# A spectral transform loop in pairs: first-stage products, second stages and mixes of two units grouped

## The chip, the cores and the metric

The kernel runs on one core of a Trainium2 chip. The metric is the device time of one execution in microseconds (us); the time given is the median of several runs. Engines are named as in the profile: PE (TensorE), DVE (VectorE), ACT (ScalarE), POOL (GpSimd) and SP (SyncE, which here issues all DMAs).

## What is computed

A spectral layer with a soft threshold, followed by a gated feed-forward network (FFN). x is 8 x 3136 x 256, the hidden width 1024, all in float32.

```python
X = np.fft.rfft(x, axis=1)
Yr = X.real @ w_r - X.imag @ w_i + b_r
Yi = X.real @ w_i + X.imag @ w_r + b_i
Y = soft(Yr, 0.01) + 1j * soft(Yi, 0.01)   # sign(v) * max(|v| - 0.01, 0)
y = np.fft.irfft(Y, n=3136, axis=1)
h = np.maximum(y @ w_in, 0)
c = depthwise convolution of h along the sequence with conv_w (3 taps)
out = (h / (1 + np.exp(-c))) @ w_out
```

## The kernel before

The sequence of 3136 is 49 x 64, and the transform goes through DRAM between its factors. The **first stage** (`stage1_pe`, L333; copies L350 on ACT and L351 on DVE; stores L338 and L342) does the 49-point part in tile products, 8 for each of the 8 batches, 64 in all; each is four matmuls with 49 x 64 weights, in the four quadrants of the PE array, into two PSUM banks. The first 8 come before the loop. The **unit** is what the loop runs over: 4 of the 24 frequencies of one batch, 6 units a batch, and two units more for an edge frequency of four batches each: 50 units, numbered 0 to 49. For each unit:

- `stage2` (L384): the 64-point part, 8 matmuls over the whole array (16 records in the profile) into two PSUM banks of the unit's `ps_s2`, from the tile a2 (L371, a DMA from the first stage's scratch). For each bank ACT copies one part (d, L387) and rounds both (fh, L388), DVE subtracts (d, L389) and takes the remainder (fl, L390). fh and fl are a value's rounded part and remainder, so that products in float32r keep float32 accuracy.
- `third`: the third plane of fh and fl, from d: ACT rounds it (L395), GpSimd takes the remainder (L396).
- `mix` (L412): the complex product with w_r and w_i in three real ones, planes 2, 0 and 1 of fh and fl in this order, 12 matmuls of 128 x 256 each (rounded x high weights, rounded x low, remainder x high), into three banks `ps_mx`; DVE adds bias and planes into v (L415, L417).
- `shrink` (L428, L429 on ACT, L430 on GpSimd) or `clip` (L422, L423 on DVE): the soft threshold, v to r.
- `stage3_pe` (L440, L443): the inverse 64-point part in quadrants, 8 matmuls (16 records), into `ps_s3`, a PSUM tile of two banks of which there is one buffer (pool psa); `stage3_out` (L450 on ACT, then a DMA store L455).

`ps_s1`, `ps_s2`, `ps_mx` and the fourth stage's tiles take their banks in turn from one pool of six (psx). The **fourth stage** (`last_stage`, `stage4`, L159, L168, L170) does the inverse 49-point part. For batch 0 its 8 pieces stand at the end of this loop; for the others they stand in the FFN.

Beside that, a generator (`background`) splits the FFN weights and taps into two float32r parts: some ten small DVE steps a piece (L264 to L280) and one ACT cast (L278). It advances one step each time it is called, three times a unit from unit 8 to 43.

The loop runs over `it` from 0 to 53 (n_it is 50, LAG 4). The order in which the code stands is the order in which each engine gets its instructions: the loop is under a manual schedule, while the FFN behind it is ordered by a scheduler. An iteration takes, in this order: the DMAs of x, tables and a2; third stage of unit it - 4; one or two first-stage products (1, 2, 1, 1, 2, 1 in turn); second stage of unit it; shrink of unit it - 2; `third` of unit it; fourth stage in iterations 45 to 48; mix of unit it - 1. Unit 49 calls `third` ahead of the shrink. Iterations 50 to 53 drain: fourth stage, third stage, clip and the last mix.

```python
psx = ab.enter_context(tc.tile_pool(name="psx", bufs=6, space=PSUM))
psa = ab.enter_context(tc.tile_pool(name="psa", bufs=1, space=PSUM))
...
            if it < n_it:
                xs[it] = stage2(items[it][1], a2s.pop(it))
...
            if 0 <= it - 1 < n_it:
                vs[it - 1] = mix(xs.pop(it - 1))
```

The FFN (from 467 us on) multiplies up (L650) and down (L678) with three float32r products each, and ACT and DVE do the gate between them.

Of the kernel before, what the change touches and what calls it, by code (L numbers as in the profile page):

```python
# [26 lines left out]
UG = 4  # L27
# [84 lines left out]
def spectral_ffn_kernel(ctx: ExitStack, tc: tile.TileContext, x, w_r, w_i, b_r, b_i,  # L112
# [61 lines left out]
    with ExitStack() as ab:  # L174
# [63 lines left out]
        def load_inv1(g):  # L238
            if g < NG:
                sl = slice(g * UG // 2, (g + 2) * UG // 2)  # L240
                nc.sync.dma_start(i1[:, 0, sl], inv1v[:, sl])
            else:
                nc.sync.dma_start(i1[:, :, U // 2], inv1v[:, U // 2:])
# [152 lines left out]
            nc.gpsimd.tensor_tensor(fl[:, :, 2], d, fh[:, :, 2].bitcast(F32), op=ALU.subtract)  # L396
            return fh, fl

        def mix(xs):


            fh, fl = xs
            ps = {c: psx.tile([K2, UG // 2, D], F32, name=f"ps_mx{c}", tag="bank") for c in (2, 0, 1)}
            for c in (2, 0, 1):
                q = (1, 2, 0)[c]
                for k in range(UG // 2):
                    mm = []
                    for t in range(NT):
                        a = [f[:, t, c, 2 * k:2 * k + 2, :] for f in (fh, fl)]
                        mm += [(a[0], wmix_hi[:, t, q, :]), (a[0], wmix_lo[:, t, q, :]), (a[1], wmix_hi[:, t, q, :])]  # L410
                    for n, (lt, rh) in enumerate(mm):
                        nc.tensor.matmul(ps[c][:, k, :], lt, rh, start=(n == 0), stop=(n == len(mm) - 1))  # L412
            v = wk.tile([K2, 2, UG // 2, D], F32, name="v")
            for c in range(2):
                nc.vector.tensor_tensor(v[:, c], ps[2], bias[:, c:c + 1, :].to_broadcast([K2, UG // 2, D]), op=ALU.add)  # L415
            for c in range(2):
                nc.vector.tensor_tensor(v[:, c], ps[c], v[:, c], op=ALU.add)  # L417
            return v

        def clip(v):  # L420
# [51 lines left out]
        LAG, WP0, LATE, NW, NF0, NF1 = 4, 8, 10, 7, 14, 3  # L472
        xs, vs, ss, a2s, xq, pair = {}, {}, {}, {}, {}, []
        p1 = nx = NX

# [8 lines left out]
        def next_s1(p):  # L484
            return stage1_pe(xq[p // 2][:, p % 2])
# [68 lines left out]
        Y0, Y1 = n_it - 6, n_it - 1  # L554
        jgs = iter(range(NPC))

        def one_by_one():
# [10 lines left out]
            stage4(jg, z2, y0, one_by_one)  # L568
            ask_z2()

        for it in range(n_it + LAG):
            drain = it >= n_it
            if it:
                fetch(1)
            if 2 < it + 2 < NG and it % 2 == 0:
                load_t2(it + 2)
            elif it == LATE:
                load_t2(NG)
                load_inv1(NG)
# [5 lines left out]
            if drain:  # L585
                last_stage()
            if it >= LAG:
                g3 = items[it - LAG]
                ps3 = stage3_pe(g3[1], ss.pop(it - LAG))
            n_s1 = min(2 if 0 < it < 5 else (1, 2, 1, 1, 2, 1)[(it - 5) % 6] if it else 0, n_pc - p1)  # L590
            ps1 = [next_s1(p1 + i) for i in range(n_s1)] if it > 1 else []
            if it >= LAG:
                stage3_out(*g3, ps3)
            if WP0 <= it < Y0:
                next(background, None)
            elif it == WP0 - 2:
                next(background)
            for ps in ps1:
                stage1_out(p1, ps)
                p1 += 1  # L600
            ask_a2(it + 1)
            if WP0 <= it < Y0:
                for _ in range(2):
                    next(background, None)
            if it < n_it:
                xs[it] = stage2(items[it][1], a2s.pop(it))
            if it == Y0:
# [6 lines left out]
            if it == n_it - 1:  # L614
                xs[it] = third(xs[it])
            if 0 <= it - 2 < n_it:
                ss[it - 2] = (clip if drain else shrink)(vs.pop(it - 2))
            if it < n_it - 1:
                xs[it] = third(xs[it])
            if Y0 < it < Y1:  # L620
                last_stage()
            if it == 1:
                for _ in range(n_s1):
                    stage1_out(p1, next_s1(p1))
                    p1 += 1
            if 0 <= it - 3 < NG:
                fill_inv1(it - 3)
            if 0 <= it - 1 < n_it:
                vs[it - 1] = mix(xs.pop(it - 1))
# [109 lines left out]
```

## Time and profile before

| | |
|---|---|
| median of 3 runs | 1681.46 us (1679.61 to 1683.54) |
| the profiled execution | 1678.42 us, span 1676.6 us |
| PE busy | 1662.8 us, 99% of the span |
| DVE busy | 1389.2 us, 83% |
| ACT busy | 1177.0 us, 70% |
| POOL busy | 192.4 us, 11%, all in the transform loop |
| mean granted PE clock | 0.997 |

Times in the trace count from the start of the span. A matmul's end is modelled and matmuls overlap, so a busy PE need not be one at its peak: what a piece of PE work costs is read from the start of its first matmul to the start of the next piece's first. A row of the timeline has start, duration, engine, line, operation, what it writes and reads, shapes, and how many equal ones follow each other (x16); in brackets the idle time before it and what ended it. The loop begins at about 33 us and its last matmul on PE is at about 467 us.

### The profile page before, as it was taken

The page shows a single profiled execution, that of the slowest core. Times are in us where ns is not written, and L with a number is a line of the kernel's source. Part 1 is how long each engine was busy: PE and PEld are TensorE (multiplying, and loading weights), DVE is VectorE, ACT ScalarE, POOL GpSimd, SP SyncE. Part 2 cuts the span into 40 slices and gives each one's busy share as a digit, 9 for nine tenths or more (in the row PEclk, how much of TensorE's full clock was granted, in tenths as well). Part 3 has the DMA queues.
Part 4 walks back from the last instruction along what each step waited for, and adds up shares of the span by engine and source line. Part 5 has one row for each costly group of instructions (what it writes and reads, how often), then busy time and mean ns, then how long its engine had stood idle before and what let it go on. Part 6 is the DMA issues. An engine that isn't in the chain of part 4 may idle for free.

```text
span 1676.6 us, 30666 instructions
## 1 busy us (share of the span) xinstructions
PE 1662.8 (99%) x12618; PEld 1543.9 (92%) x12618; DVE 1389.2 (83%) x1728; ACT 1177.0 (70%) x1585; POOL 192.4 (11%) x114
## 2 busy tenths in 40 slices
PE   9899999999999999999999999999999999999998
PEld 6788888889999999999999999999999999999998
DVE  3578888877688888888888888888888888888887
ACT  3577777777677677767676776767677676776776
POOL 1444444445300000000000000000000000000000
PEclk9899999999999999999999999999999999999999
DMA  8999999876421101111110111111001111100001
GB/s 239 279 279 291 270 261 269 254 225 186 110 79 44 49 32 42 52 52 42 52 49 26 42 39 33 42 51 52 32 33 52 52 35 49 42 23 23 23 23 45
DMA packets 108297, 162.29 MB, mean 97 GB/s; under 512 B 10842, under 2 KB 87806, under 8 KB 108094
## 3 DMA queue, kind: packets, MB, share of 16 engines
q1 hardware_dynamic: 108158, 160.34, 32.2%
q8 instruction: 100, 1.64, 0.4%
q14 instruction: 39, 0.32, 0.1%
HBM read 83.24 MB, written 77.07 MB: 96 GB/s over the span
## 4 chain that ended last, share of the span: by engine, by line
PE 97%; DMA 1%; SPq 1%; issue 1%; ACT 0%; ACTq 0%
PE ps_h L650 33%; PE acc L678 33%; PE ps_mx L412 13%; PE ps_s L159 7%; PE ps_s L384 6%; PE ps_s L333 3%; PE ps_s L440 3%; DMA hx<-in_x_dram 1%; SPq L316 0%; DMA a<-sch 0%; PE ps_s L443 0%; DMA sch<-ha 0%; SPq L319 0%; SPq L347 0%; ACT o L684 0%
## 5 line engine op out<-in xcount | busy, mean ns | idle before, releaser
L659 DVE SCALAR_TENSOR_TENSOR c<-h,cw,c 128x896 f32<-128x896 f32 x448 | 512.8, 1147 | 67.5 <-ACT c L657 66.2
L678 PE MATMUL acc<-wout,gh 128*128 128x256 f32 x3136 | 567.6, 281 | 0.4 <-ACT gh L664 0.4
L650 PE MATMUL ps_h<-yh,win 128*128 128x450 f32 x1792 | 549.1, 367 | 0.0
L678 PEld LDWEIGHTS acc<-wout,gh 128*128 128x128 f32 x3136 | 491.0, 188 | 6.4 <-ACT gh L664 0.6
L678 PE MATMUL acc<-wout,gl 128*128 128x256 f32 x1568 | 435.6, 280 | 0.0
L652 ACT ACTIVATE h<-ps_h 128x900 f32<-128x900 f32 x224 | 207.4, 926 | 234.3 <-PE ps_h L650 234.3
L650 PEld LDWEIGHTS ps_h<-yh,win 128*128 128x128 f32 x1792 | 338.7, 189 | 26.1 <-issue 0.4
L650 PE MATMUL ps_h<-yl,win 128*128 128x450 f32 x896 | 329.4, 368 | 0.0
L678 PEld LDWEIGHTS acc<-wout,gl 128*128 128x128 f32 x1568 | 293.2, 188 | 0.2
L661 DVE TENSOR_TENSOR c<-h,c 128x896 f32<-128x896 f32 x224 | 243.4, 1087 | 47.6 <-ACT c L660 46.6
L665 DVE TENSOR_TENSOR gl<-c,gh 128x896 fp32r<-128x896 f32 x224 | 243.0, 1088 | 34.4 <-ACT gh L664 30.4
L664 ACT CAST gh<-c 128x896 fp32r<-128x896 f32 x224 | 210.4, 944 | 77.0 <-DVE c L661 77.0
L660 ACT ACTIVATE c<-c 128x896 f32<-128x896 f32 x224 | 213.4, 953 | 28.4 <-DVE c L659 25.9
L650 PEld LDWEIGHTS ps_h<-yl,win 128*128 128x128 f32 x896 | 169.0, 189 | 11.3
L657 ACT ACTIVATE c<-h,cw 128x896 f32<-128x896 f32 x168 | 175.5, 1044 | 2.9 <-DVE gl L665 0.2
L412 PE MATMUL ps_mx<-wmix_hi,fh 128*128 128x256 f32 x600 | 172.5, 288 | 0.0
L412 PE MATMUL ps_mx<-wmix_lo,fh 128*128 128x256 f32 x600 | 167.9, 280 | 0.0
L412 PE MATMUL ps_mx<-wmix_hi,fl 128*128 128x256 f32 x600 | 167.4, 279 | 0.0
L430 POOL TENSOR_TENSOR r<-r,v 128x1024 f32<-128x1024 f32 x48 | 114.6, 2388 | 218.9 <-ACT v L429 200.1
L384 PEld LDWEIGHTS ps_s<-t,a 128*128 128x128 f32 (+1 forms) x800 | 94.7, 194 | 37.4 <-issue 23.3
L159 PEld LDWEIGHTS ps_s<-i,z 98*128 98x128 f32 x1024 | 122.4, 192 | 2.0 <-issue 0.8
L159 PE MATMUL ps_s<-i,z 98*128 98x98 f32 x1024 | 123.3, 273 | 0.0
(93 smaller groups left out, 1672.7 us busy)
## 6 DMA issues: line engine op xcount, KB each, us to landing
z<-sc SPq DMA_DIRECT2D x64, 392.0 KB
sc<-z SPq DMA_DIRECT2D x96, 256.0 KB
out_dram<-o SPq DMA_DIRECT2D x27, 896.0 KB
xr<-in_x_dram SPq DMA_DIRECT2D x112, 192.0 KB
sc<-a SPq DMA_DIRECT2D x56, 384.0 KB
a<-sc SPq DMA_DIRECT2D x42, 512.0 KB
hx<-in_x_dram SPq DMA_DIRECT2D x16, 192.0 KB
a<-sch SPq DMA_DIRECT2D x6, 512.0 KB
```

What stands on the lines that cost most here:

```text
L159: nc.tensor.matmul(to, z2[:, j, t * P:(t + 1) * P], i2[:, 0 if jg or j else 1, :], start=(j == 0), stop=(j == JG - 1), skip_group_check=True)
L384: nc.tensor.matmul(ps[:, k], a2[0:kk, k, t * P:(t + 1) * P], t2[0:kk, q, :], start=(k == 0), stop=(k == UG - 1), skip_group_check=True)
L412: nc.tensor.matmul(ps[c][:, k, :], lt, rh, start=(n == 0), stop=(n == len(mm) - 1))
L650: nc.tensor.matmul(ps[:, a, 0:CH + 2], lt, rh, start=(n == 0), stop=(n == len(mm) - 1))
L652: nc.scalar.activation(h, ps[:, :, 0:CH + 2], AF.Relu)
L657: nc.scalar.mul(c, h[:, :, 0:CH], cw[:, 0, f:f + 1])
L659: nc.vector.scalar_tensor_tensor(c, h[:, :, k:k + CH], cw[:, k, f:f + 1], c, op0=ALU.mult, op1=ALU.add)
L660: nc.scalar.activation(c, c, AF.Sigmoid)
L661: nc.vector.tensor_tensor(c, h[:, :, 1:CH + 1], c, op=ALU.mult)
L664: nc.scalar.copy(gh, c)
L665: nc.vector.tensor_tensor(gl, c, gh.bitcast(F32), op=ALU.subtract)
L678: nc.tensor.matmul(acc[m // 2][:, m % 2, :], lt[:, sl], rh[:, f, :], start=(f == 0 and n == 0 and m % 2 == 0), stop=(f == NF - 1 and n == ...
```

## The change

Units 0 to 7 run as before. From unit 8 on, an iteration takes units u and u + 1 (u = 8, 10, ... 48). In order: DMAs of two x loads and of a2; third stage of u - 4; up to two first-stage products; third stage of u - 3; the third product, if there is one; second stage and `third` of u, then of u + 1; shrink of u - 1; mix of u; shrink of u; mix of u + 1. Iteration 8 also does the mix of unit 7, which was left over. The six calls of `background` that two units had are spread over the pair. Iterations 46 and 48 have a fourth stage behind each second stage. In a pair's mixes (`paired`) the planes go 0, 2, 1, and the four DVE additions are regrouped: bias to planes 0 and 2 first, then plane 2 and plane 1. The drain is third stage, fourth stage, third stage and so on for units 46 to 49, and only unit 49 uses clip.

```diff
-        def mix(xs):
+        def mix(xs, paired=False):
...
-            ps = {c: psx.tile([K2, UG // 2, D], F32, name=f"ps_mx{c}", tag="bank") for c in (2, 0, 1)}
-            for c in (2, 0, 1):
+            order = (0, 2, 1) if paired else (2, 0, 1)
+            ps = {c: psx.tile([K2, UG // 2, D], F32, name=f"ps_mx{c}", tag="bank") for c in order}
+            for c in order:
...
+            if paired:
+                biased(0, 0)
+                biased(1, 2)
+                joined(0, 2)
+                joined(1, 1)
+            else:
...
-        for it in range(n_it + LAG):
+        for it in range(PAIR):
...
+        for u in range(PAIR, n_it, 2):
+            busy = u < Y0
+            fetch(2)
...
+            ask_a2(u + 2)
+            n_s1 = min(sum((1, 2, 1, 1, 2, 1)[(i - 5) % 6] for i in (u, u + 1)), n_pc - p1)
...
+            z = s3(u - LAG)
+            out1 = pieces(min(n_s1, 2))
+            next(out1)
+            if busy:
+                steps(2)
+            stage3_out(*z)
+            next(out1, None)
+            z = s3(u + 1 - LAG)
+            out1 = pieces(max(n_s1 - 2, 0))
+            next(out1)
+            stage3_out(*z)
+            next(out1, None)
+            if busy:
+                steps(1)
+            ask_a2(u + 2)
+            if u == PAIR:
+                ss[u - 2] = shrink(vs.pop(u - 2))
+                vs[u - 1] = mix(xs.pop(u - 1))
+            for i in (u, u + 1):
+                xs[i] = third(stage2(items[i][1], a2s.pop(i)))
+                if i == u:
+                    ask_a2(u + 3)
+                if u > Y0:
+                    last_stage()
...
+            ss[u - 1] = shrink(vs.pop(u - 1))
+            if busy:
+                steps(1)
+            vs[u] = mix(xs.pop(u), True)
+            ss[u] = shrink(vs.pop(u))
+            if busy:
+                steps(2)
+            vs[u + 1] = mix(xs.pop(u + 1), True)
+
+        for n in range(2):
+            z = s3(n_it - LAG + n)
+            last_stage()
+            stage3_out(*z)
+            if n == 0:
+                ss[n_it - 1] = clip(vs.pop(n_it - 1))
+            last_stage()
+        for n in range(2):
+            stage3_out(*s3(n_it - 2 + n))
```

`s3(i)` is the third stage of unit i, `pieces(n)` issues n first-stage products and, called again, their copies and stores, and `steps(n)` calls `background` n times. Two places show how the instructions move. The first is PE in the middle of the loop, before, from one third stage to the next second stage, twice (ps_s<-r is a third stage, ps_s<-xr a first-stage product, ps_s<-t a second stage; the 36 matmuls of a mix are left out between them):

```order
862 L440 MATMUL ps_s_2643<-r,i_465 64x256 x8
863 L333 MATMUL ps_s_2652<-xr,f_118 64x512 x2
864 L333 MATMUL ps_s_2653<-xr,f_118 64x512 x2
865 L333 MATMUL ps_s_2658<-xr,f_118 64x512 x2
866 L333 MATMUL ps_s_2659<-xr,f_118 64x512 x2
867 L384 MATMUL ps_s_2690<-t_122,a_2436 128x128 x4
868 L384 MATMUL ps_s_2699<-t_122,a_2436 128x128 x4
...
905 L440 MATMUL ps_s_2766<-r,i_465 64x256 x8
906 L333 MATMUL ps_s_2775<-xr,f_118 64x512 x2
907 L333 MATMUL ps_s_2776<-xr,f_118 64x512 x2
908 L384 MATMUL ps_s_2796<-t_122,a_2542 128x128 x4
909 L384 MATMUL ps_s_2805<-t_122,a_2542 128x128 x4
```

And after, from the first third stage of a pair to its last second stage; the two mixes follow:

```order
857 L453 MATMUL ps_s_2592<-r,i_465 64x256 x8
858 L333 MATMUL ps_s_2601<-xr,f_118 64x512 x2
859 L333 MATMUL ps_s_2602<-xr,f_118 64x512 x2
860 L333 MATMUL ps_s_2607<-xr,f_118 64x512 x2
861 L333 MATMUL ps_s_2608<-xr,f_118 64x512 x2
862 L453 MATMUL ps_s_2627<-r,i_465 64x256 x8
863 L333 MATMUL ps_s_2636<-xr,f_118 64x512 x2
864 L333 MATMUL ps_s_2637<-xr,f_118 64x512 x2
865 L384 MATMUL ps_s_2654<-t_122,a_2361 128x128 x4
866 L384 MATMUL ps_s_2663<-t_122,a_2361 128x128 x4
867 L384 MATMUL ps_s_2679<-t_122,a_2454 128x128 x4
868 L384 MATMUL ps_s_2688<-t_122,a_2454 128x128 x4
```

The quadrant work of two units (third and first stages) stands together, and so does the work on the whole array. The second place is ACT, before, from the copy of a third stage (z) through the second stage's copies (d, fh) and the shrink (r, v) to the third plane (fh<-d):

```order
223 L450 COPY z_2781<-ps_s_2766 128x1024
224 L350 COPY a_2674<-ps_s_2775 128x2x256
225 L387 COPY d<-ps_s_2796 128x256
226 L388 CAST fh<-ps_s_2796 128x512
227 L387 COPY d<-ps_s_2805 128x256
228 L388 CAST fh<-ps_s_2805 128x512
229 L428 ACTIVATE r<-v,small 128x1024
230 L429 ACTIVATE v<-v,small 128x1024
231 L395 CAST fh<-d 128x2x256
```

And after, from the first second stage of a pair on:

```order
363 L387 COPY d<-ps_s_4383 128x256
364 L388 CAST fh<-ps_s_4383 128x512
365 L387 COPY d<-ps_s_4392 128x256
366 L388 CAST fh<-ps_s_4392 128x512
367 L395 CAST fh<-d 128x2x256
368 L387 COPY d<-ps_s_4408 128x256
369 L388 CAST fh<-ps_s_4408 128x512
370 L387 COPY d<-ps_s_4417 128x256
371 L388 CAST fh<-ps_s_4417 128x512
372 L395 CAST fh<-d 128x2x256
373 L441 ACTIVATE r<-v,small 128x1024
374 L442 ACTIVATE v<-v,small 128x1024
```

The third plane of a unit now stands right behind its second stage, ahead of the other unit's copies and of the shrink; a second shrink and the pair's copies of third and first stages follow.

More of the change, by code (lines that the diff above doesn't have):

```diff
@@ L413, in mix, with biased, joined @@
             v = wk.tile([K2, 2, UG // 2, D], F32, name="v")
[L414 to L417, printed above, removed]
+            def biased(c, src):
+                nc.vector.tensor_tensor(v[:, c], ps[src], bias[:, c:c + 1, :].to_broadcast([K2, UG // 2, D]), op=ALU.add)
+            def joined(c, src):
+                nc.vector.tensor_tensor(v[:, c], ps[src], v[:, c], op=ALU.add)
+            if paired:
[4 more added lines that the diff above has]
+            else:
+                for c in range(2):
+                    biased(c, 2)
+                for c in range(2):
+                    joined(c, c)
             return v
@@ L553, in spectral_ffn_kernel @@
         background = later()
-        Y0, Y1 = n_it - 6, n_it - 1
+        Y0 = n_it - 6
         jgs = iter(range(NPC))
@@ L569, in last_stage, with steps, s3, pieces @@
             ask_z2()
-        for it in range(n_it + LAG):
-            drain = it >= n_it
+        def steps(n):
+            for _ in range(n):
+                next(background, None)
+        def s3(i):
+            b, g = items[i]
+            return b, g, stage3_pe(g, ss.pop(i))
+        def pieces(n):
+            nonlocal p1
+            todo = [next_s1(p1 + i) for i in range(n)]
+            yield
+            for ps in todo:
+                stage1_out(p1, ps)
+                p1 += 1
+        for it in range(PAIR):
             if it:
@@ L584, in spectral_ffn_kernel @@
                 fill_t2(it + 1)
-            if drain:
-                last_stage()
             if it >= LAG:
[L588 to L591, printed above, removed]
-            if it >= LAG:
[L593 to L597, printed above, removed]
@@ L598, in spectral_ffn_kernel @@
-            for ps in ps1:
-                stage1_out(p1, ps)
-                p1 += 1
-            ask_a2(it + 1)
[L602 to L607, printed above, removed]
+                z = s3(it - LAG)
+            n_s1 = 2 if 0 < it < 5 else (1, 2, 1, 1, 2, 1)[(it - 5) % 6] if it else 0
+            if it > 1:
+                out1 = pieces(n_s1)
+                next(out1)
@@ new lines, in spectral_ffn_kernel @@
+            if it >= LAG:
+                stage3_out(*z)
+            if it == WP0 - 2:
+                steps(1)
+            if it > 1:
+                next(out1, None)
+            ask_a2(it + 1)
+            xs[it] = stage2(items[it][1], a2s.pop(it))
+            if it >= 2:
+                ss[it - 2] = shrink(vs.pop(it - 2))
+            xs[it] = third(xs[it])
+            if it == 1:
+                out1 = pieces(n_s1)
+                next(out1)
+                next(out1, None)
+            if 0 <= it - 3 < NG:
+                fill_inv1(it - 3)
@@ L613, in spectral_ffn_kernel @@
                     ask_z2()
[L614 to L629, printed above, removed]
+            ss[u - 1] = shrink(vs.pop(u - 1))
+            if busy:
+                steps(1)
+            vs[u] = mix(xs.pop(u), True)
[6 more added lines that the diff above has]
+            last_stage()
+            stage3_out(*z)
+            if n == 0:
[3 more added lines that the diff above has]
+            stage3_out(*s3(n_it - 2 + n))
         assert p1 == n_pc and not z2s and next(background, True)
```

17 lines of the change are left out of this document (13 added, 4 removed).

## Prediction

> **What bounds the kernel now.** I read four views: the chain that ended last, TensorE's waits, the windows by stage, and then the timeline of single units, engine by engine. The page's chain puts nearly the whole span on TensorE (PE):
>
> ```profile
> PE 97%; DMA 1%; SPq 1%; issue 1%; ACT 0%; ACTq 0%
> ```
>
> PE's own waits, over the whole trace (line, releaser, total us, times, longest), are all in the first 60 us but for the fourth, 0.4 us later on; these are the first and the third:
>
> ```profile
> PE ps_s L333 <- issue: 7.1, 3, 5.4
> ...
> PE ps_s L384 <- DMA a<-sch: 0.6, 1, 0.6
> ```
>
> The windows give busy time by stage (length, PE, PE weight loads, DVE, ACT, POOL, granted clock, DMA share, GB/s):
>
> ```profile
> core 0: us, PE busy (x) PEld busy (x) DVE busy (x) ACT busy (x) POOL busy (x), PEclk, DMA share, GB/s
> ...
> 44.40:54.70 10.30, 6.97 (x27) 5.39 (x28) 5.15 (x10) 2.11 (x5) 0.84 (x2) 0.50 1.01 279
> ...
> 60.00:372.00 312.00, 312.00 (x2923) 262.35 (x2920) 258.46 (x445) 232.07 (x361) 143.92 (x79) 1.00 0.91 265
> 372.00:408.00 36.00, 36.00 (x341) 32.91 (x340) 28.72 (x55) 26.57 (x40) 17.03 (x10) 1.00 0.63 175
> ...
> 467.00:1676.60 1209.60, 1204.87 (x8290) 1160.12 (x8288) 1040.43 (x1099) 859.36 (x1072) 0.00 (x0) 1.00 0.13 41
> ```
>
> From 60 us on PE is never idle in the transform loop, DVE is at 83% (258.46 of 312) and ACT at 74%. So the change can gain only where PE itself spends time between instructions, and it can lose wherever its new order makes PE wait for another engine. The FFN part after 467 us is the same work and full of PE; I take no change there. The timeline of PE shows what a unit costs; of the mix (L412) only the ends stand here:
>
> ```profile
> 285.07 0.28 PE L412 MATMUL ps_mx<-wmix_lo,fh 128*128 128x256 f32 x1
> 285.19 0.27 PE L412 MATMUL ps_mx<-wmix_hi,fl 128*128 128x256 f32 x1
> 285.39 1.11 PE L440 MATMUL ps_s<-r,i 64*64 64x256 f32 x16
> 286.31 1.91 PE L333 MATMUL ps_s<-xr,f 49*64 49x512 f32 x16
> 288.15 2.05 PE L384 MATMUL ps_s<-t,a 128*128 128x128 f32 x16
> 289.96 0.36 PE L412 MATMUL ps_mx<-wmix_hi,fh 128*128 128x256 f32 x1
> 290.16 0.28 PE L412 MATMUL ps_mx<-wmix_lo,fh 128*128 128x256 f32 x1
> 290.27 0.28 PE L412 MATMUL ps_mx<-wmix_hi,fl 128*128 128x256 f32 x1
> ...
> 294.33 1.11 PE L440 MATMUL ps_s<-r,i 64*64 64x256 f32 x16
> 295.25 1.05 PE L333 MATMUL ps_s<-xr,f 49*64 49x512 f32 x8
> 296.23 2.05 PE L384 MATMUL ps_s<-t,a 128*128 128x128 f32 x16
> ```
>
> I read start to start: third stage 0.92, first stage 1.84 for two tile products (16 records) and 0.98 for one, second stage 1.81, mix 4.37 us (289.96 to 294.33).
>
> **What the pairing removes.** Third and first stage run in quadrants of the array (64*64), second stage and mix on all of it. Going over costs time: the last mix step to the third stage takes 0.20 (285.19 to 285.39) where two mix steps are 0.12 apart, so 0.08. A second tile product adds 1.84 - 0.98 = 0.86, so of the 0.98 of a single one 0.12 is the way back to the whole array. Units without a first stage say the same, their third stage takes 1.04 to the second stage instead of 0.92:
>
> ```profile
> 377.84 1.11 PE L440 MATMUL ps_s<-r,i 64*64 64x256 f32 x16
> 378.88 2.05 PE L384 MATMUL ps_s<-t,a 128*128 128x128 f32 x16
> ```
>
> A unit goes over and back once; a pair now does so once. 21 pairs (units 8 to 49) save 21 x (0.08 + 0.12) = 4.2 us. Second stage to second stage and mix to mix keep their usual steps, as does second stage to mix now (0.03 and 0.20 instead of 0.11 and 0.12).
>
> On this price the Trainium skill has a rule: TensorEngine Tiling, Key Properties, says that changing the tiling mode drains TensorE. The rows above show 0.08 and 0.12 us for it; a full drain is the rival that ends faster, below.
>
> **What it adds, first: the third plane is due early.** In the mix of unit u the planes are now taken in the order 0, 2, 1, right behind both second stages. Plane 2 is the longest chain: both halves of d on DVE, then its rounding on ACT (L395), then its remainder on GpSimd (L396). Before, a unit's mix came a whole unit after its second stage: here the remainder of the second stage of 288.15 starts at 295.75 and its mix at 298.04, and nobody waits.
>
> ```profile
> 295.75 1.73 POOL L396 TENSOR_TENSOR fl<-d,fh 128x512 fp32r<-128x512 f32 x1
> ```
>
> How fast that chain can be is shown by the last unit, the only one in the loop of before that runs it straight through (its third plane is called ahead of the shrink, as it now is in every pair). PE, ACT, DVE and POOL of it:
>
> ```profile
> 443.94 2.05 PE L384 MATMUL ps_s<-t,a 64*128 64x128 f32 x16
> ```
> ```profile
> 445.19 0.37 ACT L387 COPY d<-ps_s 128x256 f32<-128x256 f32 x1
> ...
> 446.29 0.59 ACT L388 CAST fh<-ps_s 128x512 fp32r<-128x512 f32 x1
> 447.52 0.62 ACT L395 CAST fh<-d 128x512 fp32r<-128x512 f32 x1 [0.64 <-DVE d L389]
> ```
> ```profile
> 446.14 0.42 DVE L389 TENSOR_TENSOR d<-ps_s,d 128x256 f32<-128x256 f32 x1 [1.45 <-ACT fh L388]
> ...
> 447.07 0.41 DVE L389 TENSOR_TENSOR d<-ps_s,d 128x256 f32<-128x256 f32 x1
> 447.41 0.68 DVE L390 TENSOR_TENSOR fl<-ps_s,fh 128x512 fp32r<-128x512 f32 x1
> ```
> ```profile
> 448.29 1.31 POOL L396 TENSOR_TENSOR fl<-d,fh 128x512 fp32r<-128x512 f32 x1 [4.43 <-ACT fh L395]
> ```
>
> From the start of the second stage: ordinary remainders ready at 4.15 (447.41 + 0.68 - 443.94), third plane at 5.66 (448.29 + 1.31 - 443.94). PE needs them so: two second stages take 2 x 1.81 = 3.62; the mix's sixth matmul, the last that newly needs an ordinary remainder, comes at 3.62 + 0.20 + 4 x 0.12 = 4.30, in time by 0.15. Plane 2's remainder is first read by the mix's 15th matmul, at 3.62 + 0.20 + 13 x 0.118 = 5.35 (0.118 from 4.37 over 36 with its ends). So PE waits 0.31 us, with a GpSimd step of 1.31. Over the loop that step was (mean ns; and from its tile, ns min/median/max):
>
> ```profile
> L396 POOL TENSOR_TENSOR fl<-d,fh 128x512 fp32r<-128x512 f32 x38 | 55.9, 1472 | 0.0
> ```
> ```profile
> L396 POOL TENSOR_TENSOR fl<-d,fh x50: 1260/1310/1747, 32.6 to 448.3; 128x512 fp32r<-128x512 f32 x50
> ```
>
> That bounds the wait by 0.26 and 0.75 us; between 1.31 (0.31) and the mean 1.47 (0.47) I take 0.40, since DVE is less busy at that moment than in the mean. Pairs 8 to 44 have nothing between second stage and mix: 19 x 0.40 = 7.6 us. In pairs 46 and 48 two fourth stages lie between and cover it. If DVE is late for the first d, all of it slips. It is wanted 2.2 us after the second stage starts (446.14 - 443.94). Ahead of it stand the copy of the third tile product and one step of the weight splitting:
>
> ```profile
> 287.45 0.69 DVE L351 COPY a<-ps_s 128x512 f32<-128x512 f32 x1 [0.31 <-PE ps_s L333]
> ```
> ```profile
> L269 DVE TENSOR_TENSOR wout_m<-wout_m,wout_e 128x512 int32<-128x512 int32 x4 | 4.0, 1010 | 0.0
> ```
>
> The copy starts 1.14 after its product (287.45 - 286.31), so DVE is free 1.14 + 0.69 + 1.01 - 0.98 = 1.86 after the second stage starts: 0.34 to spare, and a rival.
>
> **Second: two third stages share one PSUM tile.** ps_s3 has a single buffer, so the pair's second third stage waits until ACT has copied the first out:
>
> ```profile
> 379.03 1.01 ACT L450 COPY z<-ps_s 128x1024 f32<-128x1024 f32 x1 [1.68 <-PE ps_s L440]
> ```
>
> It is free 379.03 + 1.01 - 377.84 = 2.20 after the first third stage starts. With two tile products between them the second starts at 0.92 + 1.84 - 0.12 = 2.64 anyway: no wait. The tile products run out (64 in all): pair 40 has one, 0.92 + 0.86 = 1.78, a wait of 0.42; pairs 42, 44, 46 and 48 have none, 0.90, a wait of 1.30 each. Sum 4 x 1.30 + 0.42 = 5.6 us. Before, a unit followed its third stage with the second stage, which needed no such tile.
>
> **Edits at nothing.** The bias adds go in another order, the same four of 0.68 us. ACT's shrink of unit u comes behind the mix of u and is covered by the mix of u+1 (4.37). PSUM: the mix of u+1 takes the banks of the second stages, read out by 4.15, needed at about 8. On SP the x loads of a pair and the next a2 are asked together at its head and the other a2 behind the first second stage, some 17 us ahead where it was 8 to 17; z stores and a1 stores follow in the same order, and with a DMA share of 0.91 a burst may land later: 0 to 0.6 (the one DMA wait PE ever had at L384), I take 0. In the drain the clip of unit 48 becomes a shrink on ACT and POOL with two fourth stages and more ahead of its reader, and the fourth stages stand two by two with three buffers of z2 ahead of them: 0, give or take 1 us.
>
> **The sum.** -4.2 + 7.6 + 5.6 = +9.0 us. The profiled execution took 1678.4 us (span 1676.6), so it becomes 1687.4; the runs' median is 1681.5, 3.1 above the profiled one, and the forecast is 1681.5 + 9.0 = 1690.5. By the ends of the GpSimd step it is 19 x 0.26 = 4.9 to 19 x 0.75 = 14.3 instead of 7.6, so 1687.8 to 1697.2. What a measurement here can tell from no change is about 0.2%, 3.4 us.
>
> **Rivals.** *The third plane is in time* (0.20): GpSimd or the hand-over is quicker, the 7.6 falls away, 1681.5 - 4.2 + 5.6 = 1682.9, no change. For it: the miss is 0.3 of 5.7 us. Against: each step of the last unit's chain already waited for the one before.
>
> *DVE gets late* (0.17): it is at 83% over the loop and in order; if the weight steps push d by 0.4 in every pair the wait doubles to 0.80, 19 x 0.80 = 15.2, so 1698.1. Against: the 0.34 to spare.
>
> *The switch is a full drain* (0.10, ends faster): place, the two boundaries a pair no longer has. If each cost what a matmul in flight lasts, 0.27 at the mix (row of 285.19) and 0.59 at the first stage (1.05 less one step of 0.43 and 0.03 for its four quadrants), a pair saves 0.86 and 21 pairs 18.1: 1681.5 - 18.1 + 13.2 = 1676.6. It decides from 0.79 a pair on ((13.2 + 3.4) / 21). Against it stand the starts, 0.08 and 0.12.
>
> *The clock falls* (0.03): the row of 44.40 shows half clock for 10.3 us, behind the only long idle time of PE:
>
> ```profile
> 47.73 1.97 PE L333 MATMUL ps_s<-xr,f 49*64 49x512 f32 x4 [5.42 <-issue]
> ```
>
> Each such stretch costs about 5.1 us; if all four waits of 1.30 set it off, 1690.5 + 20.6 = 1711. Against: the wait that did was 5.42. The Trainium skill, TensorE: Matmul & The Clock Gate, Why this matters for your kernels, warns of idle gaps over about 3 us, which fits that row and not a gap of 1.30.
>
> **Numbers.** Forecast 0.50, at 1690.5 (its own range 1687 to 1697). Slower by over 0.2%: 0.50 + 0.17 + 0.03 = 0.70; within: 0.20; faster: 0.10. A range of 1682 to 1700 holds the forecast, the late DVE and the plane in time, and leaves out the drain and the clock.
>
> **What would show it.** Right: in TensorE's waits a line for the mix waiting on POOL fl, 19 times about 0.4 us, and one for the third stage waiting on ACT z, four times 1.3 and once 0.4; a pair with three products takes 2 x (4.37 + 0.92 + 1.81) + 1.84 + 0.98 - 0.20 + 0.40 = 17.2 us. Wrong: no PE wait on POOL (then the plane was in time), mix waits on DVE or longer ones on POOL (DVE late), a third stage waiting between tile products, or boundaries far shorter than 0.20 and 0.12 were.

## The result, and the profile after

The changed kernel takes 1708.71 us (median of 4 runs, 1704.37 to 1711.99), the kernel before 1680.53 us in the same session (1678.98 to 1683.54). The ratio is 1.0168, 95% interval 1.0151 to 1.0184: slower by 28 us. The forecast was slower, at 1690.5 us; its range ended at 1700, so the sign came out and the size did not.

TensorE's waits between 60 and 520 us, where the page of before had none longer than 0.4 us (what waited, for what; us in total, times, longest):

```profile
PE ps_s L453 <- ACT z L463: 5.4, 5, 1.2
PE ps_s L333 <- DMA xr<-in_x_dram: 4.6, 2, 2.8
PE ps_s L333 <- issue: 4.4, 2, 2.4
PE ps_mx L413 <- POOL fl L396: 2.5, 15, 0.2
PE ps_s L333 <- DVE v L417: 1.7, 2, 1.3
PE ps_s L333 <- DVE a L351: 1.2, 1, 1.2
PE ps_h L715 <- DVE yl L170: 0.5, 1, 0.5
```

The first and the fourth line are the two waits that were forecast. The second, third and sixth are new: first-stage products (L333) that wait for their tile of x, though two of these three lines are put down to something else (below). The chain that ended last, 97% on PE before:

```profile
PE 85%; ACT 2%; DVE 2%; DMA 1%; issue 1%; POOL 1%; SPq 0%; ACTq 0%; POOLq 0%; DVEq 0%
```

It now goes over other engines from time to time. The window of the changed kernel over the same 312 us of the loop:

```profile
core 0: us, PE busy (x) PEld busy (x) DVE busy (x) ACT busy (x) POOL busy (x), PEclk, DMA share, GB/s
60.00:372.00 312.00, 300.28 (x2754) 255.44 (x2754) 251.95 (x415) 221.84 (x340) 135.12 (x73) 0.99 0.91 252
```

PE, busy for all of the 312 us before, now stands idle for 11.7 of them, and its granted clock is 0.99. The DMA engines are as busy as before (0.91) and move less (252 GB/s against 265). How much the loop lost, two starts show, of unit 5's second stage (ahead of the changed code) and of the FFN's first matmul; in the profiled execution before

```profile
77.08 2.05 PE L384 MATMUL ps_s<-t,a 128*128 128x128 f32 x16
...
467.14 0.47 PE L650 MATMUL ps_h<-yh,win 128*128 128x450 f32 x1
```

and after

```profile
83.04 2.05 PE L384 MATMUL ps_s<-t,a 128*128 128x128 f32 x16
...
499.15 0.44 PE L715 MATMUL ps_h<-yh,win 128*128 128x450 f32 x1 [0.52 <-DVE yl L170]
```

From the one to the other it was 390.06 us and is 416.11: 26.0 us more in the paired loop. (The 6 us by which this execution is late at the first row arose in the unchanged start-up, while the first x loads come in; that part varies from run to run.)

Where the 26.0 us are, read start to start over all pairs of the changed kernel, each step against its undisturbed length:

| term | forecast | measured |
|---|---|---|
| array-mode changes saved (21 pairs) | -4.2 | about -7.5 |
| mix waits for the third plane on POOL (18 of 19 pairs) | +7.6 | +7.4 |
| third stage waits for the copy of ps_s3 (5 pairs) | +5.6 | +6.5 |
| a pair's third product waits for x (5 pairs) | 0 | +12.0 |
| half clock behind three of these waits | 0 | +4.8 |
| products (2 pairs, 3.8) and one mix (0.3) wait for DVE | 0 | +4.1 |
| the drain, with the FFN's first wait for DVE | 0 | -1.2 |
| sum | +9.0 | +26.1 |

Undisturbed, a third product starts 0.87 us behind its third stage and takes 1.02 us to the second stage, two second stages take 3.59 and two mixes 8.58. The mode changes are what a pair without any wait is shorter than two units before, 0.33 to 0.37 us with three products, 0.38 with two and 0.41 with none.

The two new large terms stand together. PE in the pair of units 14 and 15:

```profile
161.30 1.11 PE L453 MATMUL ps_s<-r,i 64*64 64x256 f32 x16
162.21 1.91 PE L333 MATMUL ps_s<-xr,f 49*64 49x512 f32 x16
163.93 1.09 PE L453 MATMUL ps_s<-r,i 64*64 64x256 f32 x16
167.38 1.20 PE L333 MATMUL ps_s<-xr,f 49*64 49x512 f32 x8 [2.36 <-issue]
168.52 5.47 PE L384 MATMUL ps_s<-t,a 128*128 128x128 f32 x32
```

The two products take 162.21 to 163.93, 1.72 us, exactly the forecast 1.84 - 0.12 of the saved mode change. Then PE stands idle for 2.36 us ahead of the third product, which starts 2.59 us late, and the two second stages behind it take 5.47 us instead of 3.84: the clock. SP's queue, in order, ahead of that:

```profile
151.34 1.94 SPq L468 DMA_DIRECT2D sc<-z  x2
153.39 2.01 SPq L338 DMA_DIRECT2D sc<-a  x2
...
158.74 1.96 SPq L316 DMA_DIRECT2D xr<-in_x_dram  x4
```

The x of product 30 is asked at 158.74, behind the pair before's stores, and its matmul runs at 167.38, 8.6 us later. Before, in the same place:

```profile
139.86 4.21 SPq L316 DMA_DIRECT2D xr<-in_x_dram  x4
```
```profile
159.61 1.91 PE L333 MATMUL ps_s<-xr,f 49*64 49x512 f32 x16
```

there product 30 is the second of the two in the last row (from 160.5 on), 20.6 us behind its request. The same holds for the products 38, 46, 54 and 62: from the first transfer's issue to the matmul it was 18.0 to 20.6 us in these five places and is 7.7 to 8.6 us (8.2 in the mean), with waits of 2.59, 3.01, 2.05, 1.39 and 2.25 us, start to start; the product behind the wait then takes another 0.1 to 0.2 us longer than usual, at full clock too. All other x loads of the pairs are asked 12.9 us or more ahead.

### The profile page after: what moved, and what is told of

It reads as the page before. It is cut to its first block, busy times and chain, and to the rows that moved or that the text cites. A ratio compares the mean times of both kernels' runs of the same rounds, so it can differ in the third digit from the quotient of the medians.

```text
span 1710.1 us, 30676 instructions
## 1 busy us (share of the span) xinstructions
PE 1672.5 (98%) x12618; PEld 1554.6 (91%) x12618; DVE 1392.7 (81%) x1726; ACT 1183.5 (69%) x1587; POOL 195.1 (11%) x115
## 4 chain that ended last, share of the span: by engine, by line
PE 85%; ACT 2%; DVE 2%; DMA 1%; issue 1%; POOL 1%; SPq 0%; ACTq 0%; POOLq 0%; DVEq 0%
PE ps_h L715 32%; PE acc L743 32%; PE ps_mx L413 8%; PE ps_s L159 7%; PE ps_s L384 2%; PE ps_s L453 2%; PE ps_s L333 2%; DMA xr<-in_x_dram 1%; POOL fl L396 1%; ACT fh L395 1%; DVE fl L390 0%; ACT z L463 0%; DVE d L389 0%; ACT fh L388 0%; SPq L316 0%
## 5 line engine op out<-in xcount | busy, mean ns | idle before, releaser
L443 POOL TENSOR_TENSOR r<-r,v 128x1024 f32<-128x1024 f32 x49 | 119.4, 2436 | 66.6 <-ACT v L442 48.0
L384 PEld LDWEIGHTS ps_s<-t,a 128*128 128x128 f32 (+1 forms) x800 | 99.3, 205 | 22.1 <-issue 15.5
```

The lines of the kernel that those rows point to most:

```text
L384: nc.tensor.matmul(ps[:, k], a2[0:kk, k, t * P:(t + 1) * P], t2[0:kk, q, :], start=(k == 0), stop=(k == UG - 1), skip_group_check=True)
```

## The experiments

Theory: a pair that starts on an even product (units 14, 20, 26, 32, 38) takes as its third product one whose x is asked only at that pair's own head, because the three buffers of x are full one pair earlier; SP's queue comes to it late, behind stores that wait, so the load lands late. (The pair of unit 8 starts on an even product as well, but its x was asked 20.9 us ahead, still by the unpaired iterations.) The waits add up with the two that were forecast, and an idle time of 2 us or more can also drop the clock. Rival: the DMA engines, at 0.91, have no more to give; whoever is asked first, someone else is late. Loss is given below as ratio - 1 times 1680 us: +28 for the changed kernel.

**Asking x sooner in the code.** First, behind a pair's last products (e1):

```diff
             stage3_out(*z)
             next(out1, None)
+            fetch(2)
             if busy:
                 steps(1)
```

> The changed kernel with one more request for x behind a pair's last first-stage product, so that the third product's x is asked some 12 us earlier. Theory A (late request): in pairs that start on an even product (units 14, 20, 26, 32, 38) the third product waits 11.1 us in all for an x that was asked at the head of the same pair, and three of these waits are followed by 3.4 us at half clock (about 5 us in all); both go, 1708.7 - 16 = 1693 us, give or take 3. Rival B (the DMA engines are full there, share 0.9 and more): the x lands no earlier, the waits stay or move to a2, 1706 to 1710.

1706.21 us, ratio 1.0144 (1.0126 to 1.0162), a loss of 24 us. PE's waits:

```profile
PE ps_s L384 <- DMA a<-sc: 9.6, 4, 3.5
...
PE ps_s L333 <- DMA xr<-in_x_dram: 1.0, 1, 1.0
```

The products hardly wait any more; the second stages do, for a2, whose request the x loads now stand ahead of. This speaks for the rival, or for another order on SP. So x went behind the a2 of the second unit (e5):

```diff
                 if i == u:
                     ask_a2(u + 3)
+                    fetch(2)
```

> The changed kernel with one more request for x per pair, this time behind the request for the a2 of unit u + 3, so that it stands ahead of no a2. Theory A2 (the DMAs come in time once no request stands in SP's one queue ahead of one that is due sooner): neither the third product nor a second stage waits for a DMA, no half clock in the loop, 1708.7 - 11 - 5 = 1693 us, give or take 3. Rival B (with a DMA share of 0.9 there the engines themselves cannot carry it any sooner): the waits only move again, 1703 to 1708, as in the run that asked for x earlier.

1707.64 us, ratio 1.0167 (1.0138 to 1.0195): no gain, against the expectation. The third product's x was still asked late, SP having reached it no sooner: at 152.17 for a use at 160.44 in the pair of unit 14, 8.3 us ahead. Between this place in the code and the next pair's head hardly another DMA is asked (now and then a load of weights), so on SP's queue it is the same place. To ask earlier, the request has to stand ahead of the stores, right behind the matmuls of the first two products, where a buffer is just coming free (e9):

```diff
-        def fetch(n):
+        def fetch(n, issued=0):
...
-                if nx < min(n_pc, p1 // 2 * 2 + 2 * XRB):
+                if nx < min(n_pc, (p1 + issued) // 2 * 2 + 2 * XRB):
...
             out1 = pieces(min(n_s1, 2))
             next(out1)
+            fetch(2, min(n_s1, 2))
```

> The changed kernel with the next x asked right behind the matmuls of a pair's first two products, ahead of the pair's z and a1 stores on SP's queue, so that the third product of a pair that starts on an even product finds its x asked some 20 us ahead and not 6 us. Theory (the request is late because it stands behind stores that wait): the 11.1 us of third-product waits and the 5.2 us of half clock behind them go, from 1708.7 to about 1692 (1690 to 1697). Rival (the DMA engines have no more to give, so that asking earlier only moves the wait to another transfer, as in the run that asked behind the third product): second stages wait for their own loads instead, 1703 or more.

1693.41 us, ratio 1.0080 (1.0067 to 1.0093): a loss of 13 us, so 15 of the 28 are back, where 16.3 were expected. SP and PE for the same product:

```profile
140.76 2.00 SPq L316 DMA_DIRECT2D xr<-in_x_dram  x4
```
```profile
159.33 1.09 PE L333 MATMUL ps_s<-xr,f 49*64 49x512 f32 x8
```

Asked 18.6 us ahead, it is in time, nothing stands in brackets, and the loop has no half clock. So the rival, that asking sooner only makes another transfer late, does not hold for these loads. Its longest waits on PE are the two forecast ones, 1.1 us for a2 and 1.1 us for DVE; the first three:

```profile
PE ps_s L453 <- ACT z L463: 5.4, 5, 1.2
PE ps_mx L413 <- POOL fl L396: 2.4, 15, 0.2
PE ps_s L384 <- DMA a<-sc: 1.1, 2, 0.7
```

This also settles what the page left unclear: the wait put down to "issue" and the 1.2 us put down to DVE's copy went with the same edit, so they were x as well.

**The clock by itself** (e2). The third product of a pair that starts on an even product was preceded by 48 small matmuls on constants, into the banks that it then overwrites, so that PE is busy while it waits.

```diff
-            out1 = pieces(max(n_s1 - 2, 0))
+            out1 = pieces(max(n_s1 - 2, 0), 12 if p1 % 2 == 0 else 0)
```

> The changed kernel with 48 small matmuls on a constant (some 1.3 us) into the third product's own banks, ahead of it, in the pairs where it waits for its x; the x is asked as late as before and the product overwrites what they left. Theory A with the clock as a cost of its own: the half clock behind those waits goes since PE is idle for under 2 us each time, 1708.7 - 5 = 1704. Rival C (the half clock costs nothing, or is not set off by these waits): 1708 to 1710.

1708.52 us, ratio 1.0158 (1.0140 to 1.0176). PE around the same product, and the window of the loop:

```profile
163.47 2.85 PE L359 MATMUL ps_s<-ones 64*64 64x128 f32 x96
...
167.10 3.84 PE L389 MATMUL ps_s<-t,a 128*128 128x128 f32 x32
```
```profile
60.00:372.00 312.00, 306.53 (x3209) 262.80 (x3208) 249.08 (x410) 219.75 (x338) 135.16 (x74) 1.00 0.91 249
```

The second stages are back at 3.84 us and the clock at 1.00: the half clock comes from the idle time. It cost 1.63 us (5.47 - 3.84) in two of the three stretches of the changed kernel and 1.49 in the third, 4.8 us together. The total stayed, though, where the expectation without a cost of the clock had it (1708 to 1710). The trace shows what took the gain back. The filling takes 2.6 us each time, also where x came sooner (in the pair of unit 32, whose wait was 1.4); the edit fills in the pair of unit 8 too, where nothing waited; and in the pair of unit 26 a wait of 1.4 us came on top. So the price of the clock is shown by these rows and not by the total.

**The forecast waits, one at a time.** The third plane last in the mix (e3), so that GpSimd has 12 more matmuls' time:

```diff
-            order = (0, 2, 1) if paired else (2, 0, 1)
+            order = (0, 1, 2) if paired else (2, 0, 1)
...
-                biased(1, 2)
+                biased(1, 1)
                 joined(0, 2)
-                joined(1, 1)
+                joined(1, 2)
```

> The changed kernel with the planes of a pair's mixes in the order 0, 1, 2 (and DVE's additions to match: bias to 0 and 1, then plane 2 to both). Theory A: the 17 to 19 waits of 0.3 us for GpSimd's remainder go, 5.6 us; DVE is done 0.6 us later after each mix, which is hidden: 1703, give or take 2. Rival D (DVE's later end delays the shrink and the banks of the next products): 1706 to 1712.

The second third stage of a pair without two products, moved behind the first second stage (e4; in e10, e12 and e15 further down, ahead of the fourth stage that is there in two of these pairs):

```diff
+            split = n_s1 < 2
+            if not split:
...
                 if u > Y0:
                     last_stage()
+                if split and i == u:
+                    stage3_out(*s3(u + 1 - LAG))
```

> The changed kernel with the second third stage behind the first second stage in the pairs that have fewer than two tile products (units 40 to 48). Theory A: the waits for ACT's copy of the single third-stage tile go (5.7 + 0.4 us) and five more changes between whole array and quadrants come (5 x 0.2): 1708.7 - 5 = 1703.5. Rival: the copy is late anyway, since ACT then has the second stage's copies in its queue, and the wait moves: 1707 to 1709.

And the weight's cast on ACT ahead of the shrink that it stood behind (e6), for the wait on DVE:

```diff
-            ss[u] = shrink(vs.pop(u))
             if busy:
                 steps(2)
+            ss[u] = shrink(vs.pop(u))
```

> The changed kernel with the two weight-splitting steps ahead of the shrink of u instead of behind it; DVE's order stays word for word, on ACT the cast of the weights comes ahead of that shrink. Theory E (DVE's step behind the cast sits waiting up to 3.0 us, and with it the additions that free the banks of the next products): the waits of the first products for DVE in units 18 and 24 (1.5 and 0.6 us) and part of what follows go, 2 to 4 us: 1705 to 1707. Rival: those waits are DMA waits in another place, nothing changes: 1708 to 1710.

What e6 is about shows on DVE in the changed kernel, in the pair of unit 18: the weight step waits 2.97 us for ACT's cast, and behind it stand the additions (L417) whose banks the next products need.

```profile
199.18 2.46 DVE L279 TENSOR_TENSOR win_m<-win_m,win 128x512 f32<-128x512 f32 x1 [2.97 <-ACT win L278]
...
202.28 1.28 DVE L417 TENSOR_TENSOR v<-ps_mx,bias 128x512 f32<-128x512 f32 x2
```

| run | ratio (95% interval) | loss | its wait | x on PE |
|---|---|---|---|---|
| changed kernel | 1.0168 (1.0151 to 1.0184) | 28 us | | 10.2 us |
| e3, third plane last | 1.0152 (1.0125 to 1.0179) | 26 us | gone | 12.1 us |
| e4, third stages split | 1.0112 (1.0079 to 1.0145) | 19 us | gone | 9.7 us |
| e6, cast first | 1.0182 (1.0167 to 1.0197) | 31 us | gone | 15.1 us |

("x on PE" is the sum of the lines for L333 on xr, issue and the copy a.) Each edit removed its wait from PE. e4 gained what it should and more, though its interval is wide (13 to 24 us). The other two gained nothing that can be told: what PE no longer waited for elsewhere it waited for at x. e6 shows it best; it came out no faster than the changed kernel (1.0182 against 1.0168), with 15.1 us of waits for x.

The first two and x behind a2 together (e7), and all of these with the cast first (e8):

> Three edits together: x asked behind a2, plane 2 last in the pairs' mixes, the second third stage behind the first second stage where there are fewer than two products. Theory: of the sum only the saved changes of the array's mode remain (-4.2 us, less 1 for the five pairs that change once more) and DVE's wait for the cast (+2 to 4): 1681.5 - 3 + 3 = 1681.5, give or take 3. Rival B (DMA): 1690 or more.

> The three edits and the cast ahead of the shrink. Theory: PE waits for nothing in the loop and the pairing keeps what it saves, 1681.5 - 3 = 1678.5, the first version that would not be slower than the kernel before. Rival B (DMA): 1688 or more.

1702.79 us, ratio 1.0133 (1.0109 to 1.0157), and 1698.90 us, ratio 1.0115 (1.0094 to 1.0136): losses of 22 and 19 us, and not level with the kernel before, as the theory had it. About 16 and 12 would be left if the waits that went (7.4 and 6.5, then 3.8) simply came off the 28, with the five mode changes that come back (0.36 each). In e8 PE waits for x, 16.7 us, and for nothing else in the loop but 0.5 us at the end:

```profile
PE ps_s L333 <- DMA xr<-in_x_dram: 12.0, 3, 5.0
PE ps_s L333 <- issue: 4.7, 2, 2.8
```

So as long as x is asked late, part of what any other edit takes away comes back as a longer wait for x.

**Everything, with x early** (e10: e3, e4, e6 and e9).

> The same early x, with the three other waits taken out as well: the third plane last in the mix, the second third stage of a two-product pair behind the first second stage, and the weight's cast ahead of the shrink. Theory: the waits add up once x no longer takes them over, 1708.7 - 16.3 - 5.6 - 6.3 - 2.1 = 1678.4 (1675 to 1684), level with the kernel before or some 2 us under it, since the 4.2 us of saved array-mode changes stay. Rival (DMA has no more to give): as the run with the three alone and a late x, 1696 to 1700.

1681.16 us (12 runs, 1678.31 to 1688.52), ratio 1.0017 (1.0005 to 1.0029): a loss of 3 us. Of 28 us 25 are back, to within 3 us of the 1678.4 expected. By the start-to-start terms above, with the five mode changes that come back, it should have been 1676, so some 5 us went elsewhere. What is left on PE in its profile, of an execution 5 us above the median:

```profile
PE ps_s L384 <- DMA a<-sc: 6.5, 3, 3.9
PE ps_s L384 <- ACT fh L395: 2.2, 1, 2.2
```

The second a2 of a pair now comes late, asked behind two x loads and the stores. Two more versions tried to take that away: one x ahead of the stores and not two (e12, `fetch(1, min(n_s1, 2))`), and a fourth a2 buffer on top, so that both a2 are asked at the pair's head (e15):

```diff
-        a2p = ab.enter_context(tc.tile_pool(name="a2p", bufs=3))
+        a2p = ab.enter_context(tc.tile_pool(name="a2p", bufs=4))
...
-            ask_a2(u + 2)
+            ask_a2(u + 2, u + 3)
```

> The run with all four edits, but with only one x asked ahead of a pair's stores and not two, so that the request that the other one pushes back on SP's queue, the a2 of the pair's second unit, is asked earlier. Theory (SP's queue runs late, and what stands in it first decides who waits): the 9.1 us that second stages waited for a2 in that run's profile go without the x waits coming back, 1681.2 - 6 to 9 = about 1674 (1671 to 1679), so faster than the kernel before. Rival (the transfers as such are at their limit, whoever is asked first): 1680 to 1684, with a2 or x waits of some 9 us still there.

> The run with one early x, with a fourth a2 buffer, so that both a2 of the next pair are asked at a pair's head and not the second one behind its first second stage. Theory (SP's order decides): the 4.2 us of a2 waits left in that run's profile go, and its long runs (up to 1693.7) with them: 1684.4 - 4 to 8 = about 1678 (1674 to 1681). Rival (the transfers are at their limit): 1681 to 1686, with the waits at x, z or a1 stores in place of a2.

e12 took 1684.35 us (1679.33 to 1693.66), ratio 1.0028 (1.0011 to 1.0045): not the gain that was expected, and a wider spread, though the a2 waits in its profile, of an execution 3 us below the median, were 3.9 us. e15 took 1680.85 us (1677.02 to 1687.93), ratio 1.0000 (0.9987 to 1.0012): level with the kernel before. No wait for a transfer is left in its profile; instead the mix now waits for DVE and ACT:

```profile
PE ps_mx L413 <- DVE fl L390: 2.9, 7, 0.6
PE ps_mx L413 <- ACT fh L388: 1.6, 1, 1.6
```

These are 4.5 us of idle time, in an execution 3 us above the median. No version beat the kernel before, though the saved mode changes, less the five that come back, are worth some 6 us. Whether its spread and the last waits come from DMA or from the engines was not separated.

**A late x in the old order.** The kernel before, with the x of those five products asked later. Two tries moved the code but did not make the request late. e11 put it behind the unit's stores, e13 held it back a unit, to be asked with the next x:

> The kernel before, in its own order, with five of its loads of x (for products 30, 38, 46, 54 and 62) asked at the end of a unit's stores instead of at its head, so some 6 to 9 us ahead of their use and not 16. Theory (lateness alone costs the time): each use waits about 2 us and two or three of them set off a half clock, 1680.5 + 5 x 2 + 3 x 1.7 = about 1695 if the lead falls to 6 us (1687 to 1697). Rival (it is the pair's order of work, the five transfers as such are in time even so): within 2 us of 1680.5.

> The kernel before in its own order, with the x of products 30, 38, 46, 54 and 62 held back by one unit and asked together with the next one, which puts the request some 7 us ahead of its use, as in the changed kernel (the earlier try left it where it was, at 16.5 us, since SP came to it no earlier). Theory (a request 6 to 7 us ahead lands 1.3 to 3 us too late, whatever the order of the work): 5 waits of 2 to 3 us, with half clock behind some, 1679.4 + 10 to 18 = 1689 to 1697. Rival (the pair's bunched work delays the transfer, so that 7 us are enough in the old order): within 2 us of 1679.4.

e11: 1679.92 us, ratio 1.0000 (0.9991 to 1.0009), but SP came to the request hardly later, 19.1 us ahead of the use of product 30 where it was 20.6, so it tells nothing. e13: 1679.87 us, ratio 0.9995 (0.9986 to 1.0003). In e13 the requests stood 10.6 to 12.2 us ahead of the matmul, counted from the first transfer, and none waited; as they were not under the 8.2 us that a load took in the changed kernel, this only bounds it: eleven microseconds are enough. e14 put them behind the z store:

```diff
-            if it:
+            held = {30: 14, 38: 20, 46: 26, 54: 32, 62: 38}.get(nx, 0)
+            if it and not held:
                 fetch(1)
...
             ask_a2(it + 1)
+            if it == held:
+                fetch(1)
```

> The kernel before in its own order, with the x of products 30, 38, 46, 54 and 62 held back further, behind a unit's z store. The run before this one asked it 10.6 to 12.2 us ahead of its use (from the first of its five transfers to the matmul) and nothing waited; the changed kernel's five uses came 7.7 to 8.7 us behind the request, so a load takes about 8.2 us, and only a request nearer than that can wait. Here it should stand 4 to 7 us ahead. Theory: each use comes about 8.2 us behind its request, so 5 waits of 1.5 to 4 us, with half clock behind those over about 2.4 us: 1679.9 + 8 to 25 = 1688 to 1705. Rival (loads are that slow only among the pair's bunched transfers): uses follow sooner, 1684 or less.

1685.45 us (10 runs), ratio 1.0027 (1.0015 to 1.0038): slower by 4.5 us. Product 38 on PE:

```profile
215.41 1.20 PE L333 MATMUL ps_s<-xr,f 49*64 49x512 f32 x8 [1.08 <-DMA xr<-in_x_dram]
```

The five uses came 6.7 to 7.8 us behind their requests, and four of them were 0.4 to 1.3 us late, start to start; no half clock followed. One second stage also waited, 1.2 us, put down to a weight step on DVE; its cause is open. So a late request alone costs time in the old order too. Its size lies between what theory and rival expected: here a load was in after about 7 us where it took 8.2 in the changed kernel, so the pair's bunched transfers seem to add about a microsecond to each wait.

## Why the prediction was wrong

**The step that failed** stands under "Edits at nothing": the x loads of a pair "are asked together at its head ... some 17 us ahead where it was 8 to 17", a burst "may land later: 0 to 0.6 ... I take 0". Seventeen microseconds hold for an x that is used in the next pair. The third product of a pair that starts on an even product uses one asked at its own head, about 6 us before PE gets there (start of the third product without a wait less the request: 167.38 - 2.59 - 158.74 = 6.05), and a load takes 8.2. The lead was taken as one figure for all loads; written down product by product, with the buffer limit of `fetch`, it would have shown five loads for which it is a third. Cost: 12.0 us at the third products and 4.8 us of clock behind them, 16.8 us, where 17.0 lie between the forecast 9.0 and the measured 26.0; e9 takes 15 us back by the place of the x requests on the queue. That the other terms together come out close to their forecast (26.1 - 16.8 = 9.3 against 9.0) is luck: the mode changes save more and DVE costs more than was forecast.

**The mode changes**: right in place, and 1.72 us for two products is as worked out; but a pair saves 0.33 to 0.41 us and not 0.20. The prediction let mix to mix keep its usual step. The first step of a mix behind a second stage takes 0.20 (289.96 to 290.16 before) where the others take 0.12, and a pair has that one once. Two mixes without a wait, in the pair of unit 20:

```profile
231.27 0.36 PE L413 MATMUL ps_mx<-wmix_hi,fh 128*128 128x256 f32 x1
...
239.85 1.11 PE L453 MATMUL ps_s<-r,i 64*64 64x256 f32 x16
```

They take 8.58 us to the next third stage, where 2 x 4.37 = 8.74 were taken. The rival of the full drain, which needed 0.79 a pair to show, is out.

**The third plane**: right mechanism, and right size in sum. The two pairs with a fourth stage in between are covered, as forecast; in the others it looks like this:

```profile
441.91 0.28 PE L413 MATMUL ps_mx<-wmix_lo,fh 128*128 128x256 f32 x1
442.35 0.38 PE L413 MATMUL ps_mx<-wmix_hi,fl 128*128 128x256 f32 x1 [0.16 <-POOL fl L396]
442.57 0.28 PE L413 MATMUL ps_mx<-wmix_hi,fh 128*128 128x256 f32 x1
```

From the first to the second it is 0.44 instead of 0.12, a wait of 0.32 us: the lower value of the two, 0.31 with a GpSimd step of 1.31. The step behind it takes 0.22 instead of 0.12, which the prediction did not have, so a pair loses 0.43 us; over the 19 the mean is 0.39 (7.4 / 19), since three half-clock pairs and that of unit 24 lose less. That it meets the 0.40 taken is partly luck: 0.40 was half-way to a mean from a stretch where DVE is busier. Beside the covered two, the plane was in time in one pair only, behind second stages at half clock, so that rival is out as well.

**One PSUM tile for two third stages**: right. A late pair:

```profile
433.32 1.11 PE L453 MATMUL ps_s<-r,i 64*64 64x256 f32 x16
435.67 1.11 PE L453 MATMUL ps_s<-r,i 64*64 64x256 f32 x16 [1.24 <-ACT z L463]
```

It is 2.35 us from the one to the other, where 2.20 were forecast; in sum 6.5 us against 5.6.

**DVE late**: it made one mix wait in the changed kernel, by 0.3 us (unit 10's pair), and the 15.2 us did not come. It came at another place, 3.8 us at the products of two pairs, through ACT's cast.

**The clock**: it fell, in three stretches, not behind the four waits of 1.30 to which the rival was tied, but behind waits that the forecast had at nothing. Its price was taken from a stretch of 10.3 us (5.1); these are 3.4 us long and cost 1.5 to 1.6 each. The idle time of 5.42 us that was held against the rival said nothing of shorter ones: here 2.02 us were enough. The third-stage waits of 1.24 us set nothing off in this trace, but in e4 a wait of 1.28 us did (below).

## What to carry to other kernels

When a loop is regrouped, write down for each load the lead from its place on the issuing queue to its first use, one by one, with the buffer limit that lets it go and the stores that it stands behind; an average lead hides the few that matter. A loss with several waits is not the sum of removable parts as long as one late transfer takes over part of what the others leave: take that one away first, then the others count. And a request moves only if it passes something on the queue that waits.

## What the runs showed of the hardware

**Idle time well under 3 us halves the clock, by a fixed grid.** Windows and products of the changed kernel:

```profile
168.60:172.00 3.40, 3.40 (x16) 3.40 (x17) 1.50 (x4) 1.34 (x3) 0.00 (x0) 0.50 1.07 295
...
226.60:230.00 3.40, 3.40 (x19) 3.40 (x18) 1.96 (x4) 2.04 (x6) 0.00 (x0) 0.50 1.06 345
387.10:390.50 3.40, 3.40 (x19) 3.19 (x16) 0.90 (x3) 1.45 (x3) 0.00 (x0) 0.50 0.86 304
```
```profile
224.92 1.20 PE L333 MATMUL ps_s<-xr,f 49*64 49x512 f32 x8 [2.79 <-DMA xr<-in_x_dram]
...
278.77 1.20 PE L333 MATMUL ps_s<-xr,f 49*64 49x512 f32 x8 [1.82 <-DMA xr<-in_x_dram]
...
386.08 1.30 PE L333 MATMUL ps_s<-xr,f 49*64 49x512 f32 x8 [2.02 <-issue]
```

Idle times of 2.36, 2.79 and 2.02 us were followed by a stretch of 3.4 us at half clock, one of 1.82 was not, and in e10 one of 2.23 was not either:

```profile
268.75 1.46 PE L384 MATMUL ps_s<-t,a 128*128 128x128 f32 x11 [2.23 <-ACT fh L395]
```

So length alone doesn't decide. The stretches begin 58.0 and 160.4 us apart, 17 and 47 times 3.413. Laid on that grid of windows, the idle times that halved the clock fill about 50 to 64% of one window, 2.02 us lying wholly in one, and those of 1.82 and 2.23 us fall across a border, 42% of a window at most. The Trainium skill, TensorE: Matmul & The Clock Gate, What's actually happening, has the window at 3413 ns and free-running, and the trace agrees with both; its advice, under Why this matters for your kernels, of no gaps over about 3 us is too mild by these rows, since 2.02 us were enough. A share of about half a window would separate these five, but it isn't the limit either. In e4, 1.28 us in the middle of a window, 37% of it, were followed by a half-clock stretch:

```profile
197.91 0.84 PE L333 MATMUL ps_s<-xr,f 49*64 49x512 f32 x2 [1.28 <-DVE v L417]
```
```profile
198.30:201.60 3.30, 3.30 (x25) 2.17 (x22) 3.27 (x7) 0.19 (x1) 0.00 (x0) 0.50 1.12 303
```

In e3, 2.01 us ahead of the product at 384.16, 55% of a window, were not; the clock behind them is 1.00. What decides beside the idle time stays open.

**The queue that issues the DMAs can be a bound of its own.** In the changed kernel, from 100 to 390 us, SP's longest line of waits is

```profile
SPq L468 <- ACT a L350: 35.9, 10, 6.0
```

z stores that wait for ACT, up to 6.0 us at a time, with every load asked later in the code behind them. The Trainium skill, DMA: Bandwidth & Descriptors, Anatomy of one DMA — SWDGE (gpsimd) path, says that a wait for a semaphore happens on the issuing sequencer ahead of dispatch and not in the DMA engines; the section is about DMAs that GpSimd issues. For SP, e1, e5 and e9 agree: moving the x request between places behind the stores left it 7.7 to 9.5 us ahead of its use, moving it past them made it 18.6 to 20.7 us.
